# LayerNorm statistics of three blocks on ScalarE, and an earlier load of the second GLU chunk's weights, in a Trainium2 kernel

## Chip, cores and metric

The kernel runs on one core of one Trainium2 chip. The metric is the device time of one execution in microseconds. Three runs of the kernel before gave 1589.58, 1590.20 and 1592.14 us, median 1590.2. The profile is of one execution, with a span of 1589.2 us.

## The reference

A pre-norm transformer layer in float32 with 2048 tokens of 576 values: attention in 32 heads of 18, in which each token sees itself and the seven tokens 2, 4, ... 14 places before it, then a gated MLP of width 4608.

```python
def _layernorm(x, axis=-1, eps=1e-5):
    m = jnp.mean(x, axis=axis, keepdims=True)
    v = jnp.var(x, axis=axis, keepdims=True)
    return (x - m) / jnp.sqrt(v + eps)
...
    h = x + _A_ref(_layernorm(x, axis=-1), A_wqkv, A_wo)
    h2 = h + _B_ref(_layernorm(h, axis=-1), B_w_gate, B_w_up, B_w_down)
...
    # _A_ref: W, dil = 8, 2
    idx = pos[:, None] - off[None, :]
    logits = jnp.einsum("bhsd,bhswd->bhsw", q, kg) * scale
    logits = jnp.where(mask[None, None, :, :], logits, -1e9)
    attn = _softmax(logits, axis=-1)
    o = jnp.einsum("bhsw,bhswd->bhsd", attn, vg)
    return (lambda x, *d: x.transpose(*d))(o, 0, 2, 1, 3).reshape(B, S, D) @ wo
...
    # _B_ref
    h = _sigmoid(g) * u
    return jnp.einsum("bsf,fd->bsd", h, w_down)
```

## The kernel before

The tokens are cut into four blocks of 512 (even and odd tokens, first and second half of each), and each block into four tiles of 128 tokens. Matrix products are made in a float32 form of reduced precision: each operand is split into a high and a low part, and three products are summed. `split` does that: ScalarE copies the source into the high part (line 104), VectorE subtracts it from the source for the low part (line 105); `split_rest` is the same for the last 64 of the 576 values, which are stored twice (lines 108 and 109).

Stage one is norm, q, k and v, and attention. `ln1` norms the tiles of a block with `ln_j`, TensorE transposes each (`tr_main`, line 139, and `tr_rest`, line 143), and the result is split into `th` and `tl`. In `ln_j` VectorE makes mean and variance by two `bn_stats` and a `bn_aggr` and adds EPS (lines 123 to 125), GpSimd takes the power -0.5 (line 126). For blocks 0 and 1 VectorE then subtracts and scales in one instruction (line 134) and copies the last 64 values (line 135); for blocks 2 and 3 VectorE negates the mean (line 129) and ScalarE subtracts it (centring, line 130), scales (line 131) and copies (line 132). `qkv` makes, for a block and a group of eight heads, 14 products per tile of tokens (`tok_major`, lines 150 to 153), evicted by ScalarE (line 384) and written to memory by three transfers that ScalarE issues (lines 388 and 390). `norm_under` interleaves the norm of the next block with the products of the present one, in the order in which the program text emits them, shifted by priorities (`tc.high_priority`); each engine's instructions are then in a fixed queue, and an instruction that waits holds all behind it on its engine.

Attention (`att_all`) runs on VectorE: for a pass (block, head group) it loads q, k and v windows on SyncE's queue, multiplies, reduces, takes a maximum and subtracts it (lines 182 to 195), takes the exponential on ScalarE (line 196), normalizes and sums with v (lines 208 to 219). `step(ag, n)` advances it between other work. Block 0's output stays on chip; those of blocks 1 to 3 go to memory (line 221) and come back as `oj`. `front` makes block 0's projection, second norm and the GLU operands, and stores two of them (lines 503 and 505).

Stage two is the GLU: 14 single chunks and 22 paired chunks of 128 hidden values, for blocks 0 and 1 and then for 2 and 3. `single` makes two sums, pg and pu, in two of the three banks b1 to b3, takes the sigmoid of pg on ScalarE (line 653) and multiplies on VectorE (`hidden`, line 629). Weights come with `load_gu` (line 565) and are split in `weights`; chunk 0's weights `wg` are loaded earlier and split by `first_split` into the tile `wf`. Between the stages the memory pools of stage one (`ps_stk`, `sa_stk`) are closed, and those of stage two take their place. After that, chunk 1's weights are loaded on GpSimd's queue (line 979), and chunk 0's down weights are split into a `d` tile (line 981). `under_first` runs the rest of block 1's attention, and then its projection, under the first chunks.

The pool `sah` has two buffers named `h`. They hold in turn the input x of blocks 0, 1, 2 and 3, the raw q, k and v weights of the last head group, and x of block 0 again for the residual.

Of the kernel before, what the change touches and what calls it, by code (L numbers as in the profile page):

```python
# [15 lines left out]
F32 = mybir.dt.float32  # L16
F32R = mybir.dt.float32r
AF = mybir.ActivationFunctionType
ALU = mybir.AluOpType
AX = mybir.AxisListType  # L20

P = 128
S = 2048
D = 576
# [6 lines left out]
NS = 4  # L31
TB = P * NS
DM = 512
DR = D - DM
DX = D + DR
# [5 lines left out]
EPS = 1e-5  # L41
# [3 lines left out]
GU = 10 * P  # L45
WC = GU + D
# [6 lines left out]
HI = 400  # L53
# [7 lines left out]
def kernel(ctx, tc, x, wqkv, wo, wmlp, out):  # L61
# [41 lines left out]
    def split(hi, lo, src):  # L103
        act.activation(hi, src, AF.Copy)  # L104
        splits.append(dve.tensor_tensor(lo, src, f32(hi), ALU.subtract))  # L105
# [9 lines left out]
                sp.dma_start(bass.AP(tensor=a.tensor, offset=a.offset,  # L115
                                     ap=[[LP * CG // 16, 16], [1, LP * CG // 16]]), zero)

    def ln_j(xj, xn, on_act):
        bs = sm.tile([P, 2, 6], F32, bufs=4, name="bs")
        mv = sm.tile([P, 2], F32, bufs=4, name="mv")  # L120
        rstd = sm.tile([P, 1], F32, bufs=4, name="rstd")
        for k in range(2):
            dve.bn_stats(bs[:, k], xj[:, k * DH2:(k + 1) * DH2])
        dve.bn_aggr(mv, bs)
        dve.tensor_scalar(rstd, mv[:, 1:2], EPS, None, ALU.add)
        pool.tensor_tensor(rstd, rstd, mhalf, ALU.pow)
        if on_act:
            nm = sm.tile([P, 1], F32, bufs=4, name="nm")
            dve.tensor_scalar(nm, mv[:, 0:1], -1.0, None, ALU.mult)
            act.activation(xn[:, :D], xj, AF.Identity, bias=nm)  # L130
            act.activation(xn[:, :D], xn[:, :D], AF.Copy, scale=rstd)
            act.activation(xn[:, D:DX], xn[:, DM:D], AF.Copy)
        else:
            dve.tensor_scalar(xn[:, :D], xj, mv[:, 0:1], rstd, ALU.subtract, ALU.mult)
            dve.tensor_copy(xn[:, D:DX], xn[:, DM:D])

    def tr_main(ps, xn):
        for c in range(4):
# [86 lines left out]
    def step(gen, n):  # L225
        for _ in range(n):
            if next(gen, END) is END:
                return

    def drain(gen):  # L230
        for _ in gen:
            pass
# [7 lines left out]
    def proj_j(bank, t, wos, th, tl, xn_tile, put, order=(0, 1)):  # L240
        oj = t[0]
        pv = tr_main(bank(), oj)
        with tc.high_priority(HI):
            split(th[:, 0:4], tl, pv)
        yield
        pv = tr_rest(bank(), oj)
        with tc.high_priority(HI):
            split_rest(th[:, 4], pv)
        yield
        for i in order:  # L250
            ps = bank()
            tok_major(ps, DH2, th, tl, slice(0, P), *wos[i])
            hs = t[1][:, i * DH2:(i + 1) * DH2]
            with tc.high_priority(HI):
                dve.tensor_tensor(hs, hs, ps[:, :DH2], ALU.add)
            yield
        xn = xn_tile()
        with tc.high_priority(HI):
            ln_j(t[1], xn, False)
        yield  # L260
        pv = tr_main(bank(), xn)
        with tc.high_priority(HI):
            put(pv, slice(0, 4))
        yield
        pv = tr_rest(bank(), xn)
        with tc.high_priority(HI):
            put(pv.unsqueeze(1), slice(4, 5))
        yield
# [53 lines left out]
    def tok_tile(shape=(P, NS, DX)):  # L322
        return stk.tile(list(shape), F32, tag="tok", bufs=2, name="tok")
# [14 lines left out]
    def ln1(b, xb):  # L338
        th = th3_tile(F32R) if b == 3 else th_tile()
        tl = tl_tile()  # L340
        yield th, tl
        xn = tok_tile()
        for j in range(NS):
            js = slice(j * P, (j + 1) * P)
            pri = 2 * HI if b == 0 else HI if b > 1 else 0
            with tc.high_priority(pri):
                ln_j(xb[:, j], xn[:, j], b > 1)
            pv = tr_main(mm_tile(), xn[:, j])
            pr = tr_rest(acc_tile(), xn[:, j])
            with tc.high_priority(pri):  # L350
                split(th[:, 0:4, js], tl[:, :, js], pv)
                split_rest(th[:, 4, js], pr)
            yield
# [153 lines left out]
    def first_split(ws):  # L507
        wf = xt.tile([P, 20, P], F32R, tag="th", bufs=3, name="wf")
        r = ws[:, :GU].rearrange("p (c n) -> p c n", c=10)
        parts = []  # L510
        for lo, hi, c0, c1 in ((0, 10, 5, 10), (10, 14, 3, 5), (14, 20, 0, 3)):
            t = wf[:, lo:hi].rearrange("p (a c) n -> p a c n", a=2)
            split(t[:, 0], t[:, 1], r[:, c0:c1])
            parts.append(t)
        w1, w2, w4 = parts
        return dict(b00=(w1, 0), b10=(w1, 2), b01=(w2, 0), g4=(w1, 4), u4=(w4, 0), b11=(w4, 1))
# [2 lines left out]
    fr = front()  # L519
    for _ in qkv(1, 3, T[1], w[3]):  # L520
        step(ag, 1 if ready else 4)
    while not ready:
        step(ag, 1)
    more = qkv(2, 3, T[2], w[3])
# [15 lines left out]
                ww = first_split(wg)  # L540
    with tc.high_priority(HI):
        drain(fr)
    ps_stk.close()
    sa_stk.close()

# [17 lines left out]
    def load_gu(f, eng=sp, n=WC):  # L563
        ws = gw.tile([P, WC], F32, bufs=2, name="wg")
        behind[0] = eng.dma_start(ws[:, :n], wmlp[f][:, :n])
        return ws
# [5 lines left out]
    def d_tile():  # L572
        return gd.tile([P, 2, D], F32R, bufs=4, name="d")
# [401 lines left out]
    items = ([("std", 0, f) for f in range(NSTD)] + [("pair", 0, f) for f in range(NSTD, NF)]  # L975
             + [("std", 1, f) for f in range(NSTD)] + [("pair", 1, f) for f in range(NF)])
    bg = under_first()
    with tc.high_priority(2 * HI):
        wg2 = load_gu(1, pool)
        d = d_tile()  # L980
        split(d[:, 0], d[:, 1], wg[:, GU:WC])
        wc = ww, d
    wg = wg2
    seg = []

    def last_pair(i):
# [123 lines left out]
    for c, (kind, p, f) in enumerate(items):  # L1110
        w, d = wc
        for b, late_c in ((0, NF + NSTD - 3), (1, NF + NSTD + 5)):
            if c == late_c:
                e, hf = BLOCKS[b]
                paced(ov[e, hf], hacc[b])
        skip = () if kind == "std" else (3,)
        by_seven = c >= NF + NSTD
        if c == NSTD:
            finish_bg()
            last_x = splits[-1]  # L1120
            bg = under_rest(getattr(last_x, "ins", last_x))
        if c == NF + NSTD:
            finish_bg()
            with tc.high_priority(HI):
                for n in ("s1", "a11"):
                    Xn[n] = x_half(*raw[n])
            X = Xn
            pp_stk.close()
            dw = ctx.enter_context(sb_pool("dw", "right"))
        if c + 1 < len(items):  # L1130
            wc = weights(items[c + 1][0], wg, c + 1 < NF + NSTD)
        if c + 2 < len(items):
            wg = load_gu(items[c + 2][2], n=WC if c + 2 < NF + NSTD else GU)
        hid = {}
        blocks = [p] if kind == "std" else [2 * p, 2 * p + 1]

        def last(h0, h1):
            hid[0] = hidden(*h0, "h0")
            hid[1] = hidden(*h1, "h1")

        if kind == "std":
            hid = single(X, w, p, late, twice)
        elif not by_seven:
            side = last_pair if c == NF - 1 else bg_step

            def between(i):
                if i in (4, 6):
                    units(2)
                side(i)

            pair(X, w, between, last)
        else:
            def between(i):
                nonlocal st, gc, gc_bufs, dk
                units(1)
                if c == NF + NSTD and i == 5:
                    assert not queue
                    st_stk.close()
                    gc_stk.close()
                    gc = gc_stk.enter_context(sb_pool("gc2"))  # L1160
                    st = st_stk.enter_context(sb_pool("st2"))
                    dk = dk_stk.enter_context(sb_pool("dk", "right"))
                    for n in ("s4h", "s4l", "s1h"):
                        dk.tile([P, TB], F32R, name=n)
                    gc_bufs = 2
                down_side(f, i)

            pair(X, w, between, last if f >= NF - NPL else last_sums(f))
            if f < NF - NPL:
                if f % 2:  # L1170
                    if f == 1:
                        queue.append(lag(LAG))
                    queue.append(seven())
                continue
            d = M[f]
        seg.append((hid, d))
        if len(seg) == 2:
            if by_seven and f == NF - NPL + 1:
                queue.append(load_tails())
            for b in blocks:  # L1180
                queue.append(down_std(seg, b, f // 2) if kind == "std" else
                             down_tail(seg, b, f == NF - 1) if by_seven else down_units(seg, b))
            seg = []
# [44 lines left out]
```

## Time and profile before

| | us |
|---|---|
| median of the runs | 1590.2 |
| span of the profiled execution | 1589.2 |
| TensorE busy | 1553.3 |
| VectorE busy | 1268.1 |
| ScalarE busy | 869.2 |
| GpSimd busy | 184.2 |
| first product of GLU chunk 0 starts | 222.95 |

PE is TensorE's matrix products, PEld its weight loads, DVE VectorE, ACT ScalarE, POOL GpSimd, SP SyncE; a q behind the name (ACTq, SPq) marks the issue of a transfer by that engine's queue. A line such as `L609 PE MATMUL b<-tl,w` tells the line of the program, the engine, the operation, and which tile is written from which. In brackets stands how long the engine was idle before the instruction and what ended the wait. "Granted clock" is the share of TensorE's full clock that the chip granted. Matrix products overlap, so the duration of one is longer than the time from its start to the next one's start.

### The profile page before, as it was taken

How to read it: one execution, taken by the hardware profiler on the slowest of the kernel's cores; microseconds unless marked ns; L12 is line 12 of the kernel's file. 1: busy time of each engine (PE TensorE's matmuls, PEld its weight loads, DVE VectorE, ACT ScalarE, POOL GpSimd, SP SyncE). 2: the span in 40 equal slices, each digit the busy share in tenths (PEclk: the TensorE clock that was granted, in tenths of full speed). 3: DMA queues.
4: the chain of work that ended last, by engine and by line, in shares of the span. 5: the costliest groups of instructions: out<-in, count | busy, mean ns of one | idle time of the engine just before them, and what ended most of it. 6: DMA issues, size and time to landing. Idle time of an engine off the chain costs nothing.

```text
span 1589.2 us, 22383 instructions
## 1 busy us (share of the span) xinstructions
PE 1553.3 (98%) x8532; PEld 1381.6 (87%) x8532; DVE 1268.1 (80%) x1931; ACT 869.2 (55%) x1546; POOL 184.2 (12%) x230
## 2 busy tenths in 40 slices
PE   7999979999999999999989999999999999999998
PEld 6999968888888888888879988888888888888887
DVE  7999988959999999999546687876677776677755
ACT  4432234425555666656443255776677776677761
POOL 1000000011010001000101100122112112212210
PEclk9999999999999999999999999999999999999999
DMA  7664544346367565665764234899989999989983
GB/s 267 208 206 163 193 184 165 133 177 246 104 164 205 157 170 139 166 191 149 210 203 143 100 110 110 182 186 181 176 169 183 184 173 180 177 170 182 184 170 124
DMA packets 76892, 273.50 MB, mean 172 GB/s; under 512 B 8336, under 2 KB 14224, under 8 KB 75888
## 3 DMA queue, kind: packets, MB, share of 16 engines
q0 software_dynamic: 27792, 105.89, 36.3%
q1 hardware_dynamic: 41360, 146.06, 27.4%
q10 hardware_dynamic: 7632, 20.12, 3.3%
q8 instruction: 67, 1.10, 0.3%
q14 instruction: 41, 0.34, 0.1%
HBM read 145.88 MB, written 128.52 MB: 173 GB/s over the span
## 4 chain that ended last, share of the span: by engine, by line
PE 55%; issue 27%; POOL 7%; DVE 6%; DMA 4%; ACT 1%; SPq 0%; POOLq 0%; ACTq 0%; DVEq 0%
PE b L609 23%; PE dp L723 15%; POOL h L794 7%; PE acc L150 6%; PE b L616 4%; PE b L150 1%; PE bgp L150 1%; DMA wg<-in_wmlp_dram 1%; DVE pr L182 1%; DMA x<-tok 1%; DVE pr L208 1%; DVE lg L186 1%; PE acc L152 1%; DMA tail<-h 1%; PE acc L153 1%
## 5 line engine op out<-in xcount | busy, mean ns | idle before, releaser
L609 PE MATMUL b<-tl,w 128*128 128x512 f32 x1716 | 438.1, 395 | 9.1 <-ACT w L104 6.5
L609 PEld LDWEIGHTS b<-tl,w 128*128 128x128 f32 x1716 | 311.7, 189 | 66.5 <-ACT w L104 7.7
L609 PE MATMUL b<-th,w 128*128 128x512 f32 x1368 | 352.8, 393 | 0.4 <-DVE s L698 0.3
L609 PEld LDWEIGHTS b<-th,w 128*128 128x128 f32 x1368 | 249.8, 188 | 46.7 <-DVE s L698 0.7
L104 ACT ACTIVATE w<-wg 128x640 fp32r<-128x640 f32 (+2 forms) x197 | 117.0, 598 | 125.2 <-PE b L616 59.8
L791 ACT ACTIVATE ev<-dp 128x576 f32<-128x576 f32 x224 | 145.0, 647 | 61.8 <-PE dp L785 58.2
L616 PE MATMUL b<-th,w 128*128 128x512 f32 x572 | 177.0, 391 | 0.0
L794 POOL DMA_DIRECT2D h<-ev x128 | 110.2, 862 | 456.8 <-ACT ev L791 440.5
L105 DVE TENSOR_TENSOR w<-wg,w 128x640 fp32r<-128x640 f32 (+2 forms) x197 | 126.8, 649 | 38.7 <-ACT w L104 38.3
L150 PE MATMUL acc<-qw,th 128*128 128x432 f32 x512 | 155.7, 365 | 1.2 <-DVE th L109 0.9
L105 DVE TENSOR_TENSOR w<-tw,w 128x512 fp32r<-128x512 f32 x116 | 79.6, 687 | 81.1 <-ACT w L104 80.2
L616 PEld LDWEIGHTS b<-th,w 128*128 128x128 f32 x572 | 107.7, 188 | 23.1
L723 PE MATMUL dp<-d,h0h 128*128 128x288 f32 x640 | 119.0, 296 | 1.7 <-DVE tail L733 1.7
L723 PE MATMUL dp<-d,h1h 128*128 128x288 f32 x640 | 120.0, 297 | 0.0
L723 PEld LDWEIGHTS dp<-d,h0h 128*128 128x128 f32 x640 | 99.4, 189 | 5.5 <-DVE tail L733 2.0
L150 PEld LDWEIGHTS acc<-qw,th 128*128 128x128 f32 x512 | 97.2, 190 | 6.5 <-DVE th L109 1.1
L723 PEld LDWEIGHTS dp<-d,h1h 128*128 128x128 f32 x640 | 99.5, 190 | 2.9
L731 ACT ACTIVATE stage<-dp 128x576 f32<-128x576 f32 x96 | 61.7, 646 | 62.4 <-PE dp L723 62.3
L104 ACT ACTIVATE w<-tw 128x512 fp32r<-128x512 f32 x116 | 72.8, 628 | 41.3 <-PE b L609 40.9
L150 PE MATMUL acc<-qw,tl 128*128 128x432 f32 x256 | 92.8, 362 | 0.0
L384 ACT ACTIVATE ev<-acc 128x432 f32<-128x432 f32 x64 | 33.9, 531 | 104.4 <-PE acc L153 97.7
L182 DVE TENSOR_TENSOR pr<-kw,q 128x2304 f32<-128x2304 f32 x32 | 81.7, 2552 | 2.8 <-DMA kw<-k 2.6
(278 smaller groups left out, 2899.8 us busy)
## 6 DMA issues: line engine op xcount, KB each, us to landing
h<-ev POOLq DMA_DIRECT2D x96, 576.0 KB, 7.2
wg<-in_wmlp_dram SPq DMA_DIRECT2D x49, 928.0 KB, 5.2
h<-stage POOLq DMA_DIRECT2D x24, 1152.0 KB, 10.6
wg<-in_wmlp_dram SPq DMA_DIRECT2D x36, 640.0 KB, 4.1
kw<-k SPq DMA_DIRECT2D x16, 792.0 KB, 4.4
vw<-v SPq DMA_DIRECT2D x16, 792.0 KB, 5.5
wd<-in_wmlp_dram SPq DMA_DIRECT2D x18, 576.0 KB, 7.2
h<-ev POOLq DMA_DIRECT2D x32, 288.0 KB, 6.8
```

The source lines that it names most:

```text
L104: act.activation(hi, src, AF.Copy)
L105: splits.append(dve.tensor_tensor(lo, src, f32(hi), ALU.subtract))
L150: pe.matmul(ps[:, :n], a[:, c, js], m[:, c], start=k == 0, stop=False)
L152: pe.matmul(ps[:, :n], th[:, 4, js], wh[:, 4], start=False, stop=False)
L182: dve.tensor_tensor(pr, both(kw, u), q[:, us].unsqueeze(2).broadcast_to([P, 2, W, CG]), ALU.mult)
L384: act.activation(ev[:, :, j], ps[:, :NQ].rearrange("p (t c) -> p t c", t=3), AF.Copy)
L609: pe.matmul(ps, wt[:, a, k0 + c], xx[:, m + c], start=first and k == 0, stop=k == 5, skip_group_check=True)
L616: pe.matmul(ps, wt[:, a, k0], xx[:, 4], start=False, stop=a == 1, skip_group_check=True)
L723: pe.matmul(ps[:, i, :DH2], a[:, js], d[:, m, i * DH2:(i + 1) * DH2], start=k == 0, stop=k == n)
L731: act.activation(hv, ps, AF.Copy)
L791: act.activation(hs[:, k % 2], ps[:, :, :DH2], AF.Copy)
L794: pool.dma_start(hsev[:, u, k0:k + 1], hs[:, :k + 1 - k0], accum_op=ALU.add, max_dma_last_dim=8 * D)
```

## The change

Two parts. In the first, `ln_j` keeps only the form in which VectorE does all, and is used for block 0 and for the second norm. Blocks 1, 2 and 3 take `ln_stats` and `ln_scale`: ScalarE copies x scaled by -1/576 with a sum over the row (the accumulator output), which is the negative mean; adds it to x; squares the result with a sum, which is the variance, and writes the squares over x; GpSimd adds EPS and takes the power; ScalarE scales and copies the last values. Statistics are emitted one tile ahead of the scaling. In the second, chunk 1's weights are loaded into an `h` buffer by SyncE, before the rest of block 0's work; both chunks' gate and up weights and both down weights are split before the pools are changed (`first_split`, `first_down`), and the load on GpSimd's queue is gone.

```diff
-    def ln_j(xj, xn, on_act):
+    def ln_j(xj, xn):
...
-        if on_act:
-            nm = sm.tile([P, 1], F32, bufs=4, name="nm")
-            dve.tensor_scalar(nm, mv[:, 0:1], -1.0, None, ALU.mult)
-            act.activation(xn[:, :D], xj, AF.Identity, bias=nm)
-            act.activation(xn[:, :D], xn[:, :D], AF.Copy, scale=rstd)
-            act.activation(xn[:, D:DX], xn[:, DM:D], AF.Copy)
-        else:
-            dve.tensor_scalar(xn[:, :D], xj, mv[:, 0:1], rstd, ALU.subtract, ALU.mult)
-            dve.tensor_copy(xn[:, D:DX], xn[:, DM:D])
+        dve.tensor_scalar(xn[:, :D], xj, mv[:, 0:1], rstd, ALU.subtract, ALU.mult)
+        dve.tensor_copy(xn[:, D:DX], xn[:, DM:D])
+
+    def ln_stats(xj, xn):
+        mv = sm.tile([P, 2], F32, bufs=4, name="mv")
+        nm, var = mv[:, 0:1], mv[:, 1:2]
+        rstd = sm.tile([P, 1], F32, bufs=4, name="rstd")
+        act.activation(xn[:, :D], xj, AF.Copy, scale=-1.0 / D, accum_out=nm)
+        act.activation(xn[:, :D], xj, AF.Identity, bias=nm)
+        act.activation(xj, xn[:, :D], AF.Square, scale=D ** -0.5, accum_out=var)
+        pool.tensor_scalar(rstd, var, EPS, None, ALU.add)
+        pool.tensor_tensor(rstd, rstd, mhalf, ALU.pow)
+        return rstd
+
+    def ln_scale(rstd, xn):
+        act.activation(xn[:, :D], xn[:, :D], AF.Copy, scale=rstd)
+        act.activation(xn[:, D:DX], xn[:, DM:D], AF.Copy)
...
     def ln1(b, xb):
...
+        pri = 2 * HI if b == 0 else HI if b > 1 else 0
+        rstd = []
+
+        def stats(n):
+            with tc.high_priority(pri):
+                for j in range(len(rstd), n):
+                    rstd.append(ln_stats(xb[:, j], xn[:, j]))
+
         for j in range(NS):
             js = slice(j * P, (j + 1) * P)
-            pri = 2 * HI if b == 0 else HI if b > 1 else 0
+            if b:
+                stats(min(j + 2, NS))
             with tc.high_priority(pri):
-                ln_j(xb[:, j], xn[:, j], b > 1)
+                if b:
+                    ln_scale(rstd[j], xn[:, j])
+                else:
+                    ln_j(xb[:, j], xn[:, j])
...
     for _ in qkv(1, 3, T[1], w[3]):
         step(ag, 1 if ready else 4)
+    with tc.high_priority(HI):
+        wg1 = sah.tile([P, NS, D], F32, bufs=2, name="h").rearrange("p j d -> p (j d)")[:, :WC]
+        sp.dma_start(wg1, wmlp[1])
...
     with tc.high_priority(HI):
         drain(fr)
+
+    def first_down(ws):
+        d = xt.tile([P, 2, D], F32R, tag="tl", bufs=4, name="df")
+        split(d[:, 0], d[:, 1], ws[:, GU:WC])
+        return d
+
+    with tc.high_priority(HI):
+        wc = ww, first_down(wg)
+        wc_next = first_split(wg1), first_down(wg1)
     ps_stk.close()
     sa_stk.close()
...
-    with tc.high_priority(2 * HI):
-        wg2 = load_gu(1, pool)
-        d = d_tile()
-        split(d[:, 0], d[:, 1], wg[:, GU:WC])
-        wc = ww, d
-    wg = wg2
...
-        if c + 1 < len(items):
+        if c == 0:
+            wc = wc_next
+        elif c + 1 < len(items):
             wc = weights(items[c + 1][0], wg, c + 1 < NF + NSTD)
```

More of the change, by code (lines that the diff above doesn't have):

```diff
@@ L258, in proj_j @@
         with tc.high_priority(HI):
-            ln_j(t[1], xn, False)
+            ln_j(t[1], xn)
         yield
```

## The prediction

> **What bounds the kernel now.** I read the busy table first, then the stretches, then the list of TensorE's waits.
>
> ```profile
> PE 1553.3 (98%) x8532; PEld 1381.6 (87%) x8532; DVE 1268.1 (80%) x1931; ACT 869.2 (55%) x1546; POOL 184.2 (12%) x230
> ```
>
> TensorE works 1553.3 of 1589.2 us and the change takes no matmul away, so a gain can come only from the 36 us in which it stands still, and from stretches in which it works at a lower clock. The stretches (columns: length, then busy time and instructions of TensorE, weight loads, VectorE, ScalarE, GpSimd; granted clock; DMA share; GB/s):
>
> ```profile
> 30.00:40.00 10.00, 10.00 (x59) 9.40 (x58) 6.28 (x23) 8.72 (x20) 2.62 (x5) 1.00 0.98 343
> 40.00:50.00 10.00, 9.14 (x54) 8.49 (x53) 9.72 (x29) 6.75 (x16) 2.20 (x4) 1.00 0.90 322
> 50.00:184.00 134.00, 133.74 (x695) 127.37 (x694) 128.54 (x119) 42.40 (x92) 0.91 (x1) 1.00 0.53 183
> 223.00:236.00 13.00, 6.51 (x29) 5.02 (x27) 8.63 (x5) 3.85 (x6) 1.33 (x2) 0.86 0.93 353
> 236.00:249.00 13.00, 10.46 (x30) 8.01 (x31) 9.09 (x13) 5.45 (x10) 0.00 (x0) 0.62 0.22 73
> 320.00:324.00 4.00, 4.00 (x23) 3.70 (x21) 2.05 (x3) 1.20 (x2) 0.00 (x0) 0.63 1.05 405
> 400.00:780.00 380.00, 380.00 (x2091) 336.49 (x2091) 362.22 (x455) 223.08 (x366) 32.65 (x31) 1.00 0.62 161
> ```
>
> From 30 to 40 us TensorE is never idle and ScalarE, where the change puts work, is already busy 8.72 of 10 us. From 50 to 184 both TensorE (133.74 of 134) and VectorE (128.54) are full: a delay of TensorE ahead of this stretch is not made good in it, and less work on VectorE doesn't shorten it. From 223 to 249, the passage to the GLU stage, TensorE has 9 us of idle and a clock of 0.62. From 400 to 780 it is never idle, so a shift that stands at 400 goes to the end. The waits between 200 and 330 us (us in all, times, longest):
>
> ```profile
> PE b L609 <- ACT w L104: 6.5, 1, 6.5
> PE b L609 <- DVE s L629: 2.5, 1, 2.5
> PE b L139 <- DMA oj<-o: 2.4, 1, 2.4
> ```
>
> The first two are the passage; the third is block 1's projection, which waits until its attention has been written out and read back.
>
> **Part one, the norm on ScalarE.** What VectorE loses: its group of the first 60 us (count, busy us and mean ns), then the views of the tiles mv and rstd (least, median and most ns of one):
>
> ```profile
> L123 DVE BATCH_NORM_STATS2 bs<-h 128x6 f32<-128x288 f32 x32 | 13.1, 437 | 4.5 <-DMA h<-in_x_dram 4.4
> ```
>
> ```profile
> L124 DVE BATCH_NORM_AGGREGATE mv<-bs x16: 151/200/209, 4.6 to 44.9; 128x2 f32<-128x12 f32 x16
> ```
>
> ```profile
> L125 DVE TENSOR_SCALAR rstd<-mv x16: 135/145/156, 5.0 to 45.8; 128x1 f32<-128x1 f32 x16
> L126 POOL TENSOR_TENSOR rstd<-rstd,mhalf x16: 549/552/822, 5.3 to 46.0; 128x1 f32<-128x1 f32 x16
> L134 DVE TENSOR_SCALAR tok<-h,mv,rstd x8: 562/575/580, 8.4 to 32.5; 128x576 f32<-128x576 f32 x8
> L131 ACT ACTIVATE tok<-tok,rstd x8: 764/774/778, 33.1 to 53.5; 128x576 f32<-128x576 f32 x8
> ```
>
> 24 x 0.437 + 12 x 0.200 + 20 tiny ones x 0.145 + block 1's 4 x 0.575 = 18.1 us, and block 1's four small copies. This is off TensorE's path (VectorE's stretch above); its worth is that block 1's attention ends earlier.
>
> ScalarE's queue is worked strictly in order, so what counts is where the 36 added activations stand. The rows that give the prices:
>
> ```profile
> 41.08 0.33 ACTq L388 DMA_DIRECT2D q<-ev  x1
> 41.44 0.45 ACTq L390 DMA_DIRECT2D k<-ev  x1
> 41.93 0.47 ACTq L390 DMA_DIRECT2D v<-ev  x1
> 43.56 0.53 ACT L384 ACTIVATE ev<-acc 128x432 f32<-128x432 f32 x1 [2.03 <-PE acc L153]
> 43.99 0.60 ACT L104 ACTIVATE th<-mm 128x512 fp32r<-128x512 f32 x1
> 44.49 0.27 ACT L108 ACTIVATE th<-acc 128x128 fp32r<-128x128 f32 x1
> 44.65 1.44 ACT L130 ACTIVATE tok<-h,nm 128x576 f32<-128x576 f32 x2
> ```
>
> One 128x576 activation has its result after 0.77 (L131) and holds the queue for 0.67, since two in a row end after 1.44. From start to start an eviction holds it 0.43, a wide split 0.50, a narrow one 0.16, and the three issues of q, k and v 1.3 (41.08 to the end of 41.93 + 0.47). TensorE at the same time:
>
> ```profile
> 36.75 0.60 PE L139 MATMUL mm<-ident,tok 128*128 128x128 f32 x4
> ...
> 40.05 0.60 PE L139 MATMUL mm<-ident,tok 128*128 128x128 f32 x4
> ```
>
> The transposes at 36.75 and 40.05 are those of block 1's third and fourth tile. Now they wait for nothing, because VectorE normed them early. In the changed order they wait for ScalarE's scaling.
>
> Third tile. Its scaling stands behind the eviction of the very product that ends as these transposes begin, with a square of block 2, a wide split and two narrow ones between: 0.43 + 0.67 + 0.16 + 0.50 + 0.16 + 0.77 = 2.7 after it, and I add 0.5 for the hand-overs from TensorE to ScalarE and back, an estimate: TensorE idles 3.2. The copy to the last 64 columns comes behind one more activation: 0.3.
>
> Fourth tile. After the next 14 matmuls ScalarE has, between their eviction and the scaling that the transposes want: the eviction 0.43, a scaling of block 2 0.67, the three DMA issues 1.3, a copy 0.16, a centring 0.67, a narrow split 0.16, a square 0.67, the scaling 0.77: 4.8, with 0.3 for the hand-overs 5.1 of idle. Its last-columns copy stands behind one more scaling of block 2: 0.7. Behind the waiting scaling stand the splits that VectorE's halves need, so nothing overtakes.
>
> Clock. After the idle of 2.4 us the trace grants 0.63 for 4 us (320 to 324): 4 x 0.37 = 1.5 us lost. Twice: 3.0. Together 3.2 + 0.3 + 5.1 + 0.7 + 3.0 = 12.3; the 0.9 that TensorE stands still now between 40 and 50 falls in the same place and goes: 11.4. For small waits of blocks 2 and 3, and for the fourth weight group's split, which slips in VectorE's order against TensorE, I take 1.5 (bounds 0 and a whole 2.55 product of attention, as the passage below shows it).
>
> Not shown by this trace: an activation with an accumulator output (24 of them) and GpSimd's addition of EPS. An accumulator's extra lies between 0 and 0.27, a whole narrow activation (44.49 above); about six lie on the chain of each of the two stalls. I take 0.1 each, 1.0 in all; bounds 0 and 3. The addition ahead of the power costs up to another 0.55 on GpSimd (L126); it is covered as long as ScalarE's own chain is later, which it is at both stalls. Part one puts the end of qkv later by 11.4 + 1.5 + 1.0 = 13.9, bounds 8 and 19.
>
> **Part two, the passage.**
>
> TensorE, then ScalarE, then VectorE (start, us):
>
> ```profile
> 222.95 1.56 PE L609 MATMUL b<-tl,wf 128*128 128x512 f32 x6
> ...
> 236.03 1.22 PE L609 MATMUL b<-tl,w 128*128 128x512 f32 x2 [6.52 <-ACT w L104]
> ```
>
> ```profile
> 232.36 0.68 ACT L104 ACTIVATE d<-wg 128x576 fp32r<-128x576 f32 x1 [8.68 <-DMA x<-tok]
> 232.37 0.33 ACTq L390 DMA_DIRECT2D v<-ev  x1
> 233.06 1.28 ACT L653 ACT_TABLE_LOAD   x1
> 234.36 0.60 ACT L653 ACTIVATE s<-b 128x512 f32<-128x512 f32 x1
> ```
>
> ```profile
> 223.60 2.55 DVE L182 TENSOR_TENSOR pr<-kw,q 128x2304 f32<-128x2304 f32 x1
> 226.19 2.55 DVE L186 TENSOR_REDUCE lg<-pr 128x128 f32<-128x2304 f32 x1
> ...
> 243.12 0.61 DVE L194 TENSOR_REDUCE mx<-lg 128x32 f32<-128x256 f32 x1
> ...
> 244.32 0.41 DVE L195 TENSOR_TENSOR lg<-lg,mx 128x256 f32<-128x256 f32 x1
> ```
>
> Chunk 0 takes 222.95 to 229.5 (236.03 - 6.52), 6.5 us. Chunk 1 needs as much and a wait of 2.5 follows in it. In the stretch from 236 TensorE is busy 10.46 of 13 at a clock of 0.62, and little more than a chunk's worth of products is done in it: 13 - 6.5 = 6.5 lost there, 2.5 of it idle and about 4 to the clock; with the 6.5 before it 13.0 are lost. The weights come by GpSimd's queue and their split stands on ScalarE behind a down-weight split that waits for a store (8.68).
>
> Changed, chunk 1's weights and both down splits are ready before. The bank of its first product is still held until chunk 0's sigmoid has read it, and that is late next: in ScalarE's new order it stands behind the exponential of attention's pass (1, 2), which stands behind VectorE's second product, reduce, maximum and subtraction, and these come after the new down splits. From about 1.6 after chunk 0's start (two splits of 0.75): 2.55 + 2.55 + 0.61 + 0.41, the exponential some 0.4 (an estimate: half as many elements a row as a 512 split, whose row is at 0.60), table 1.28, sigmoid 0.60 = 8.4, so 10.0; TensorE is done at 6.5 and idles 3.5, then loses between 1.5 and 4 at the lower clock; I take 2.3, nearer the single wait of 320: 5.8 in place of 13.0. Gain 7.2, bounds 4 (if the hidden multiply behind VectorE's long product, 2.55, is waited for as well) and 9. The early load waits on SyncE's queue for the raw weights of the last head group to be split, and the loads of attention's next q, k and v stand behind it; VectorE has work from the pass before, so I count nothing, at worst part of one 2.55 product.
>
> **Later.** VectorE has 18 us less to do and TensorE reaches block 1's projection about 7 later: the wait of 2.4 for the attention's last output, and the 1.5 of low clock after it, go: 3.9 (bounds 0 and 3.9).
>
> The Trainium skill, "TensorE: Matmul & The Clock Gate", section "What's actually happening", says that the clock halves only after an idle window of about 3.4 us. By that rule the 2.4 us wait would cost no clock, and the gain here would be 2.4, the whole 1.5 worse. The trace disagrees, 0.63 after 2.4 us of idle, and I go by the trace.
>
> **Sum.** Against the profiled 1589.2: + 13.9 - 7.2 - 3.9 = + 2.8, and + 1.0, part of one 2.55 product, because the evictions of q, k and v come later on ScalarE, so attention's first loads too, and its first product stands ahead of block 1's splits on VectorE: 1593.0. The median of the runs stands 1.0 above the profile's span: 1594.0.
>
> **Rivals.** (a) The norm keeps ahead: the hardware's order leaves ScalarE enough slack that the third tile's scaling is done in time, and only half of the early loss comes. For it: ScalarE idles 2.03 before 43.56. Against: that idle is a wait for TensorE's product, which the scaling would stand behind too. With 5 instead of 14.9: 1590.2 + 5 - 11.1 = 1584; with no loss at all 1579. Chance 0.22. (b) It cancels: early loss of 9 to 13 with the gains as worked out, 1588 to 1593. Chance 0.25. (c) Forecast, 1593.4 to 1599: chance 0.33. (d) Slower by more: each accumulator holds ScalarE's queue for the full 0.27 and the next step waits for it; it decides once both stalls are longer by some 2 us. Early loss 19, the passage gains only 4, the rest 3.9: 1590.2 + 19 - 7.9 = 1601. For it: ScalarE is at 8.72 of 10 where the work is added. Against: it idles at the start of the stretch. Chance 0.20. That the weights aren't early after all is excluded by the order: the load stands ahead of attention's pass (0, 3) on SyncE.
>
> **Numbers.** A measurement tells 0.2% (3.2 us) from no change. Faster is (a), 0.22; same is (b), 0.25; slower (c) and (d), 0.53. The range 1583 to 1604 takes in most of (a) and (d), and (c) alone is 1593 to 1599.
>
> **What would show it.** Waits of TensorE's transposes for ScalarE's scaling of about 3 and 5 us between 36 and 52; the start of chunk 0 near 237; one wait of about 3.5 for chunk 0's sigmoid in place of 6.5 and 2.5; no wait for oj. Wrong would be no wait before 50 us, or a long one for the hidden multiply after 240.

## The result and the profile after

The changed kernel took 1601.48 us (median of 5 runs, 1595.12 to 1604.14) against 1590.23 us before (5 runs, 1589.58 to 1592.14): ratio 1.0062, 95% interval 1.0044 to 1.0081, slower by 11.2 us. It also spreads more, 9 us against 2.6. The forecast was 1594, with a range of 1583 to 1604: the sign and the range hold, the size is off by 7.5 us. The profiled execution (1603.51 us, the second longest of the five) has a span of 1601.6 us, 12.4 more than before.

The busy table:

```profile
PE 1558.2 (97%) x8532; PEld 1385.1 (86%) x8532; DVE 1256.3 (78%) x1867; ACT 887.1 (55%) x1604; POOL 191.0 (12%) x241
```

VectorE lost 11.8 us of work net, ScalarE gained 17.9. TensorE is busy 4.9 us longer with the same matmuls, and the stretches show where its clock was lower; the other 7.5 us of the 12.4 are idle time. The stretches (columns as before):

```profile
36.00:54.00 18.00, 10.19 (x36) 8.27 (x35) 15.99 (x16) 14.35 (x36) 3.58 (x10) 0.72 0.74 266
54.00:80.00 26.00, 21.89 (x114) 20.10 (x114) 21.91 (x23) 17.32 (x45) 9.56 (x8) 0.93 0.37 127
80.00:146.00 66.00, 66.00 (x343) 63.20 (x342) 63.30 (x62) 21.43 (x46) 0.94 (x1) 1.00 0.49 177
146.00:200.00 54.00, 52.94 (x270) 50.33 (x270) 40.00 (x37) 12.58 (x26) 0.00 (x0) 1.00 0.55 196
200.00:234.00 34.00, 30.76 (x198) 29.19 (x197) 31.27 (x60) 7.77 (x21) 2.45 (x4) 0.95 0.47 167
```

Where TensorE had no idle from 30 to 40, it now stands still for 7.8 of 18 us at a clock of 0.72, for another 4.1 up to 80, and for 1.1 and 3.2 later on the way to the GLU. The timeline of TensorE names what ended these waits:

```profile
39.43 0.65 PE L147 MATMUL mm<-ident,tok 128*128 128x128 f32 x4 [3.02 <-ACT tok L142]
...
49.30 1.12 PE L147 MATMUL mm<-ident,tok 128*128 128x128 f32 x4 [4.43 <-ACT tok L142]
...
67.67 0.60 PE L158 MATMUL acc<-qw,th 128*128 128x432 f32 x1 [1.33 <-ACT ev L404]
...
74.85 0.47 PE L158 MATMUL acc<-qw,th 128*128 128x432 f32 x1 [1.97 <-ACT ev L404]
...
147.84 0.66 PE L158 MATMUL acc<-qw,th 128*128 128x432 f32 x2 [1.06 <-DVE qw L105]
...
206.55 0.40 PE L158 MATMUL mm<-wo,th 128*128 128x288 f32 x1 [2.62 <-DVE tl L105]
...
244.00 1.55 PE L641 MATMUL b<-tl,wf 128*128 128x512 f32 x6
...
254.38 1.95 PE L641 MATMUL b<-tl,wf 128*128 128x512 f32 x6 [3.85 <-ACT s L685]
...
262.47 0.62 PE L641 MATMUL b<-tl,w 128*128 128x512 f32 x2
...
319.80 0.66 PE L147 MATMUL b<-ident,oj 128*128 128x128 f32 x4 [0.33 <-DMA oj<-o]
```

L142 is the scaling in `ln_scale`, L404 the eviction of q, k and v, L685 the sigmoid. Chunk 0 starts at 244.00 instead of 222.95: 21.05 us lost. Chunk 2 starts at 262.47; before it was 248.81:

```profile
248.81 0.84 PE L609 MATMUL b<-tl,w 128*128 128x512 f32 x3
```

So the passage takes 18.5 us instead of 25.9 and gives 7.4 back. Of the 21.05 us, 13.7 are then still missing. By the end of the span another 1.3 are regained; the wait for oj is among these gains (0.33 instead of 2.40).

### The profile page after: what moved, and what is told of

Same layout as the page of the kernel before. It is cut to its first block, busy times and chain, and to the rows that moved or that the text cites. A ratio compares the mean times of both kernels' runs of the same rounds, so it can differ in the third digit from the quotient of the medians.

```text
span 1601.6 us, 22374 instructions
## 1 busy us (share of the span) xinstructions
PE 1558.2 (97%) x8532; PEld 1385.1 (86%) x8532; DVE 1256.3 (78%) x1867; ACT 887.1 (55%) x1604; POOL 191.0 (12%) x241
## 4 chain that ended last, share of the span: by engine, by line
PE 80%; DVE 10%; DMA 5%; ACT 2%; issue 1%; POOL 1%; SPq 0%; ACTq 0%; DVEq 0%; POOLq 0%
PE b L641 40%; PE dp L755 14%; PE dp L817 11%; PE b L648 7%; PE acc L158 3%; DVE lg L194 2%; DMA wg<-in_wmlp_dram 1%; DVE pr L216 1%; DVE pr L190 1%; PE b L158 1%; PE bgp L158 1%; DMA kw<-k 1%; DMA ar<-x 1%; DVE w L105 1%; DVE pr L222 1%
## 5 line engine op out<-in xcount | busy, mean ns | idle before, releaser
L641 PE MATMUL b<-tl,w 128*128 128x512 f32 x1704 | 431.3, 393 | 0.0
L641 PEld LDWEIGHTS b<-tl,w 128*128 128x128 f32 x1704 | 308.1, 188 | 55.2 <-DVE s L661 0.3
L641 PE MATMUL b<-th,w 128*128 128x512 f32 x1356 | 349.2, 392 | 1.8 <-DVE s L730 1.7
L641 PEld LDWEIGHTS b<-th,w 128*128 128x128 f32 x1356 | 246.7, 188 | 47.5 <-DVE s L730 2.1
L104 ACT ACTIVATE w<-wg 128x384 fp32r<-128x384 f32 (+2 forms) x194 | 115.4, 598 | 119.5 <-PE b L648 60.1
L158 PE MATMUL acc<-qw,th 128*128 128x432 f32 x512 | 159.5, 373 | 5.2 <-ACT ev L404 4.1
L105 DVE TENSOR_TENSOR w<-wg,w 128x384 fp32r<-128x384 f32 (+2 forms) x194 | 125.3, 651 | 37.9 <-ACT w L104 37.5
L648 PEld LDWEIGHTS b<-th,w 128*128 128x128 f32 x568 | 106.7, 188 | 23.3
L755 PE MATMUL dp<-d,h0h 128*128 128x288 f32 x608 | 112.5, 295 | 0.8 <-DVE tail L765 0.8
L190 DVE TENSOR_TENSOR pr<-kw,q 128x2304 f32<-128x2304 f32 x32 | 81.7, 2554 | 24.6 <-DMA kw<-k 24.3
L755 PEld LDWEIGHTS dp<-d,h0h 128*128 128x128 f32 x608 | 93.6, 189 | 3.8 <-DVE tail L765 1.0
L404 ACT ACTIVATE ev<-acc 128x432 f32<-128x432 f32 x64 | 33.9, 530 | 94.5 <-PE acc L161 90.8
```

The lines of the kernel that those rows point to most:

```text
L158: pe.matmul(ps[:, :n], a[:, c, js], m[:, c], start=k == 0, stop=False)
L190: dve.tensor_tensor(pr, both(kw, u), q[:, us].unsqueeze(2).broadcast_to([P, 2, W, CG]), ALU.mult)
L404: act.activation(ev[:, :, j], ps[:, :NQ].rearrange("p (t c) -> p t c", t=3), AF.Copy)
L641: pe.matmul(ps, wt[:, a, k0 + c], xx[:, m + c], start=first and k == 0, stop=k == 5, skip_group_check=True)
L648: pe.matmul(ps, wt[:, a, k0], xx[:, 4], start=False, stop=a == 1, skip_group_check=True)
L755: pe.matmul(ps[:, i, :DH2], a[:, js], d[:, m, i * DH2:(i + 1) * DH2], start=k == 0, stop=k == n)
```

## The experiments

Each time is a median of its runs, each ratio stands against runs of the kernel before taken with it. Their median is 1589.16 for early_weights_only, norm_only, block1_first and eps_in_square (one instruction on GpSimd); 1589.56 for block1_on_vector, block1_on_vector_eps (the same with one instruction), three_gpsimd and early_weights_held (early weights and the order on VectorE); and 1589.76 for before_held, changed_held (that order on the kernels before and changed) and best_norm. "Chunk 0" and "chunk 2" are the starts of their first products in the profiled execution, which is one execution of each kernel. Such starts differ between executions: changed_held (below) has TensorE's products in the same order as the changed kernel up to chunk 0, and its chunk 0 starts at 240.73, 3.3 us earlier than 244.00. The changed kernel's wait of 2.62 us at 206.55 is missing there.

### The early weights alone

The kernel before with the second part of the change only: `wg1`, `first_down` and `wc_next` as in the diff above, `ln_j` and `ln1` untouched.

> The norm as in the kernel before, chunk 1's weights and both down splits early as in the changed one. Theory A: the passage gains about 7.3 us (chunk 2 starts some 18.5 us after chunk 0 instead of 25.9), but block 1's attention is no earlier on VectorE except for the 4.3 us of idle that VectorE has in the passage before, so the wait for oj grows from 2.4 to some 4 to 6 us: 1586 to 1588. Rival B, the passage's gain is whole whatever VectorE does: 1582 to 1583. Rival C, the oj wait takes all of it: 1590.

1583.27 us (1581.79 to 1583.61), ratio 0.9957 (0.9945 to 0.9970). Chunk 0 starts at 222.96 as before, chunk 2 at 242.91: the passage takes 19.9 us, a gain of 5.9, 1.4 short of the 7.3 expected. TensorE's timeline of this kernel, and VectorE's:

```profile
237.05 2.92 PE L621 MATMUL b<-tl,wf 128*128 128x512 f32 x6 [4.38 <-DVE s L641]
```

```profile
230.59 2.55 DVE L182 TENSOR_TENSOR pr<-kw,q 128x2304 f32<-128x2304 f32 x1
233.06 0.75 DVE L105 TENSOR_TENSOR df<-h,df 128x576 fp32r<-128x576 f32 x1
233.73 2.55 DVE L186 TENSOR_REDUCE lg<-pr 128x128 f32<-128x2304 f32 x1
236.31 0.69 DVE L641 TENSOR_TENSOR s<-s,b 128x512 f32<-128x512 f32 x1
```

Here the sigmoid was in time, and the hidden multiply of chunk 0 (L641) was late: it stands on VectorE behind a product, a split and a reduce of attention. The wait for oj was 2.2 us, as before, not longer as theory A had it, and the time fell to rival B's figure: 1583. The passage's gain came through to the end without any relief on VectorE.

### The norm alone

The changed kernel with the weights loaded and split as before, by GpSimd's queue after the pool change.

> The norm statistics on ScalarE as changed, chunk 1's weights on GpSimd's queue after the pool change as before. Theory A: chunk 0 starts some 21 us later than before, the passage costs its 25.9 us as before (waits of about 6.5 and 2.5), the wait for oj goes (3.9): about 1590 + 21 - 4 = 1607. Rival: the late start is made good in part in the passage, because VectorE is ahead: 1600 or less.

1603.98 us (1601.85 to 1604.36), ratio 1.0086 (1.0073 to 1.0100). Chunk 0 starts at 241.35 and chunk 2 at 261.3, so the passage took 20.0 us and not 25.9, with a wait of 3.9 for the weights where before it was 6.5: part of the late start is made good there even without the early load. The wait for oj was 3.15 us: VectorE's relief (12.4 us less busy than before) did not remove it. The time lies between the two expectations. The norm costs 14.8 us alone; the early load is worth 5.9 us alone, and by the medians only 2.5 on top of the norm (1603.98 to 1601.48), which is inside the spread of the changed kernel's runs.

### Block 1 ahead in ScalarE's queue

```diff
-        pri = 2 * HI if b == 0 else HI if b > 1 else 0
+        pri = HI if b > 1 else 2 * HI
```

> As changed, with the norm of block 1 at block 0's priority (the same instructions in another order on ScalarE). Theory A, the order on ScalarE's queue costs the third and fourth tile's waits: they go, chunk 0 starts about 11 us earlier than in the changed kernel (near 233), and the time is about 1592 (10 off, 1 to 2 given back at oj). Rival, it is the amount of ScalarE's work, not its order: the waits come for other instructions and the time stays within 3 us of the changed kernel's 1601.

1597.17 us (1593.97 to 1597.68), ratio 1.0042 (1.0029 to 1.0054): between the two. The waits of the third and fourth tile are gone: nothing over 0.6 us until 62, and the order was their cause. Others took their place:

```profile
62.68 0.66 PE L147 MATMUL mm<-ident,tok 128*128 128x128 f32 x4 [3.05 <-ACT tok L142]
...
194.34 0.69 PE L147 MATMUL mm<-ident,tok 128*128 128x128 f32 x2 [2.48 <-DVE tok L227]
...
199.52 0.88 PE L151 MATMUL acc<-ident,tok 128*128 128x128 f32 x3 [4.06 <-DVE tok L429]
```

The first is a tile of a later block, whose scaling is late in its turn; the other two are block 0's attention, whose output (L227, L429) now comes later than TensorE wants it. Chunk 0 starts at 237.44, 6.6 us earlier than in the changed kernel, not 11.

### Block 1 back on VectorE

```diff
-            if b:
+            if b > 1:
                 stats(min(j + 2, NS))
...
-                if b:
+                if b > 1:
                     ln_scale(rstd[j], xn[:, j])
```

> As changed, with block 1 normed by VectorE as before; blocks 2 and 3 keep their statistics on ScalarE, and chunk 1's weights are early. Theory A, what costs is ScalarE's queue under block 1, and GpSimd held by VectorE's products under blocks 2 and 3: no waits of 3 and 4.4 us between 36 and 52, the start of chunk 0 near 232 (9 later than before instead of 21), 1588 to 1592. Rival, blocks 2 and 3 lose as much in any order: 1597 or more.

1600.60 us (1598.31 to 1601.56), ratio 1.0066 (1.0053 to 1.0080): the rival's case. Chunk 0 starts at 242.18, not near 232. Block 1's norm was early, but what follows it waits:

```profile
44.46 0.47 PE L158 MATMUL acc<-qw,th 128*128 128x432 f32 x1 [4.20 <-ACT th L104]
50.28 1.11 PE L147 MATMUL mm<-ident,tok 128*128 128x128 f32 x4 [5.36 <-DVE tl L105]
```

On ScalarE the splits of block 1 have no raised priority and stand behind the statistics of block 2, which have it. From 27.99 to 43.83 that queue holds evictions, transfers and nothing but block 2's norm, and the first split of block 1 comes at 43.83. The second wait, 5.36, is for VectorE's half of that split: it starts at 49.54, behind a reduce, a product and a reduce of attention that fill VectorE from 41.77 on. In each of these three orders (changed, block 1 first, block 1 on VectorE) the norm's chain on ScalarE delays something TensorE needs next.

### One, two and three instructions on GpSimd

ScalarE's scaling waits for GpSimd, and the cause shows in the changed kernel's timelines of GpSimd, VectorE and ScalarE:

```profile
49.05 0.57 POOL L138 TENSOR_TENSOR rstd<-rstd,mhalf 128x1 f32<-128x1 f32 x1
...
60.55 2.40 POOL L137 TENSOR_SCALAR rstd<-mv 128x1 f32<-128x1 f32 x1 [1.56 <-ACT h L136]
63.04 0.57 POOL L138 TENSOR_TENSOR rstd<-rstd,mhalf 128x1 f32<-128x1 f32 x1
...
70.49 2.12 POOL L137 TENSOR_SCALAR rstd<-mv 128x1 f32<-128x1 f32 x1 [2.42 <-ACT h L136]
```

```profile
47.58 2.55 DVE L194 TENSOR_REDUCE lg<-pr 128x128 f32<-128x2304 f32 x1
...
60.32 2.56 DVE L216 TENSOR_TENSOR pr<-vw,lg 128x2304 f32<-128x2304 f32 x1
...
69.98 2.56 DVE L190 TENSOR_TENSOR pr<-kw,q 128x2304 f32<-128x2304 f32 x1
```

```profile
60.52 0.67 ACT L134 ACTIVATE tok<-h 128x576 f32<-128x576 f32 x1
61.09 0.19 ACT L134 ACTIVATION_READ_ACCUMULATOR tok<-h 128x1 f32 x1
61.19 0.51 ACT L404 ACTIVATE ev<-acc 128x432 f32<-128x432 f32 x1
63.64 0.78 ACT L142 ACTIVATE tok<-tok,rstd 128x576 f32<-128x576 f32 x1 [1.94 <-POOL rstd L138]
...
64.95 0.77 ACT L135 ACTIVATE tok<-h,mv 128x576 f32<-128x576 f32 x1
65.62 0.25 ACT L143 ACTIVATE tok<-tok 128x64 f32<-128x64 f32 x1
...
73.30 0.77 ACT L142 ACTIVATE tok<-tok,rstd 128x576 f32<-128x576 f32 x1 [2.24 <-POOL rstd L138]
...
74.28 0.52 ACT L404 ACTIVATE ev<-acc 128x432 f32<-128x432 f32 x1
```

GpSimd's addition over 128 values took 2.40 us: it ended with the VectorE product that had started just before it (60.32 + 2.56 = 62.88; 60.55 + 2.40 = 62.95). The next one, 2.12 us long, did the same (69.98 + 2.56 = 72.54; 70.49 + 2.12 = 72.61). Under a reduce of the same length (47.58 to 50.13) the power took its 0.57. ScalarE waited 1.94 and 2.24 for the results, with the splits and evictions behind: the eviction at 74.28 is the one for which TensorE waits 1.97 us at 74.85. The Trainium skill, "SBUF — State Buffer", section "Who interferes with whom", says that a VectorE instruction with two inputs in SBUF contends with GpSimd's reads, that the one issued first keeps the other out for its whole length, and that a reduce never contends. The trace agrees: 2.40 and 2.12 us behind products, 0.57 under a reduce. To price it, one kernel has one instruction a tile and one has three:

```diff
+    beps = cst.tile([P, 1], F32, name="beps")
+    pool.memset(beps, (EPS / D) ** 0.5)
...
-        act.activation(xj, xn[:, :D], AF.Square, scale=D ** -0.5, accum_out=var)
-        pool.tensor_scalar(rstd, var, EPS, None, ALU.add)
-        pool.tensor_tensor(rstd, rstd, mhalf, ALU.pow)
+        act.activation(xj, xn[:, :D], AF.Square, bias=beps, scale=D ** -0.5, accum_out=var)
+        pool.tensor_tensor(rstd, var, mhalf, ALU.pow)
```

> As changed, without GpSimd's addition: EPS comes as a bias of sqrt(EPS/576) into the square, whose sum over a centred row is then the variance plus EPS. One GpSimd instruction a tile instead of two. Theory A, GpSimd's small instructions are held while VectorE's 2.55 us products run and ScalarE's scaling waits for them (1.67, 1.94 and 2.24 us in the changed kernel): about half of the 6 us that chunk 0's start loses between 54 and 80 us goes, 1597 to 1599. Rival, the evictions there are late only because ScalarE has more to do: no change, 1601.

```diff
-        pool.tensor_scalar(rstd, var, EPS, None, ALU.add)
+        pool.tensor_scalar(rstd, var, EPS / 2, None, ALU.add)
+        pool.tensor_scalar(rstd, rstd, EPS / 2, None, ALU.add)
```

> As changed, with EPS added in two halves by two GpSimd instructions: three a tile instead of two. Theory A, each of them can be held by a running VectorE product, and ScalarE's scaling waits for it: chunk 0 starts 3 to 6 us later than in the changed kernel and the time is 1604 to 1607. Rival, they cost their own 0.2 us on an idle engine: the same 1601 within 1.

One instruction: 1598.88 us (1595.74 to 1600.08), chunk 0 at 238.54. Three: 1603.26 (1602.21 to 1606.01), chunk 0 at 243.22. The medians go the way of theory A, 2.6 less and 1.8 more than the changed kernel's 1601.48, but its own runs reach from 1595 to 1604, so neither step alone is clear of the spread, and three instructions didn't start chunk 0 later than two (244.00). One against three is clear: 4.4 us, without overlap, or 2.2 us an instruction, less than I had set. The hold is shown by the rows. That it alone makes the 4.4 us is not: from 54 to 80 us TensorE idles 3.5, 4.1 and 4.4 us with one, two and three instructions, and the granted clock is 1.00, 0.93 and 0.83, so most of the difference there is clock. One instruction is held too: in that kernel the power at 67.76 takes 1.97 us, and TensorE waits 3.47 for an eviction that stands behind it on ScalarE.

With block 1 back on VectorE, where GpSimd's instructions for blocks 2 and 3 were not held up to 70 us (0.22 for each addition, 0.57 for each power), the same step does nothing:

> As block1_on_vector, with EPS as a bias in the square, so that GpSimd has one instruction a tile. Theory A: 2 to 3 us less than block1_on_vector. Rival, GpSimd's instructions don't matter: the same time as block1_on_vector.

1599.93 us (1599.06 to 1601.25) against 1600.60: no difference, the rival's figure, and it fits the hold: what is not held costs nothing. (In the profiled executions chunk 0 starts 2.1 us earlier, at 240.06; the idle time from 54 to 80 us is about the same, 3.3 and 3.5 us, and the clock is 1.00 instead of 0.91.)

### The order on VectorE in the passage

Attention's second product of pass (1, 2) waits until chunk 0's hidden multiply has been issued:

```diff
+    opened = []
...
         for u in range(2):
             us = slice(2 * u, 2 * u + 2)
+            held = (b, g, u) == (1, 2, 1)
+            while held and not opened:
+                yield
             pr = at.tile([P, 2, W, CG], F32, name="pr")
-            dve.tensor_tensor(pr, both(kw, u), q[:, us].unsqueeze(2).broadcast_to([P, 2, W, CG]),
-                              ALU.mult)
+            with ExitStack() as way:
+                if held:
+                    way.enter_context(tc.issue_after(getattr(opened[0], "ins", opened[0])))
+                dve.tensor_tensor(pr, both(kw, u),
+                                  q[:, us].unsqueeze(2).broadcast_to([P, 2, W, CG]), ALU.mult)
...
     def hidden(sg, ps, name):
-        dve.tensor_tensor(sg, sg, ps, ALU.mult)
+        opened.append(dve.tensor_tensor(sg, sg, ps, ALU.mult))
```

On top of the early weights alone:

> As early_weights_only, with attention's second product of pass (1, 2) held on VectorE until chunk 0's hidden multiply is done. In early_weights_only TensorE idled 4.4 us for that multiply, which stood behind a product and a reduce of 2.55 us each. Theory A: the idle and its low clock go (chunk 2 starts some 15 to 16 us after chunk 0 instead of 19.9), the held product and reduce come later for oj, whose wait grows from 2.2 to 4 or 5: 1580 to 1582. Rival, VectorE's sum of work decides and the order only shifts where TensorE waits: 1583, as early_weights_only.

1575.49 us (1574.21 to 1577.50), ratio 0.9912 (0.9899 to 0.9926): 14 us faster than before and the fastest of all. More than theory A gave. TensorE passes from chunk to chunk with one short wait:

```profile
235.49 0.61 PE L635 MATMUL b<-th,wf 128*128 128x512 f32 x2
236.56 1.67 PE L628 MATMUL b<-tl,w 128*128 128x512 f32 x6 [0.45 <-ACT s L672]
```

```profile
313.83 0.66 PE L139 MATMUL b<-ident,oj 128*128 128x128 f32 x4 [0.66 <-DMA oj<-o]
```

Chunk 2 starts 13.4 us after chunk 0 (223.20 to 236.56), which is two chunks of 6.4 and little else; the wait for oj did not grow, it fell to 0.66. On the kernel before, and on the changed one:

> The kernel before with attention's second product of pass (1, 2) held until chunk 0's hidden multiply, and nothing else. Theory A, early weights and the order on VectorE need each other: chunk 1 still waits 6.5 for its weights, during which the multiply is done anyway, so only the wait of 2.5 can go: 1586 to 1590. Rival, the order on VectorE alone made the 8 us between early_weights_only and early_weights_held: 1581 or less.

> As changed, with the same product held. In the changed kernel TensorE idled 3.85 us for chunk 0's sigmoid, which stood on ScalarE behind the exponential of that pass. Theory A: the exponential comes after the sigmoid, the idle and its low clock go, chunk 2 starts 14 us after chunk 0 instead of 18.5: 1595 to 1598; what the norm costs is then the difference to early_weights_held, some 20 us. Rival, VectorE's load makes another wait of the same size in its place: 1601.

Before with the hold alone: 1589.00 us (12 runs, 1586.51 to 1591.55), ratio 0.9994 (0.9985 to 1.0003), no difference: the wait for weights, 6.9 us, stays, the one of 2.5 goes, and the wait for oj is 3.4 instead of 2.4. Changed with the hold: 1594.89 (11 runs, 1591.43 to 1598.63), ratio 1.0031 (1.0018 to 1.0043); the wait for the sigmoid is gone and chunk 2 starts 12.7 us after chunk 0. Against early_weights_held the norm then costs 19.4 us. Both times came as theory A had it, the second's passage 1.3 us shorter than put there.

### The norm with all that helped

> The norm statistics on ScalarE with all that helped so far: block 1's norm at block 0's priority, EPS in the square, chunk 1's weights early, the product held. Theory A, statistics on ScalarE cost more than VectorE's relief is worth in any of these orders: 1585 to 1592, at least 10 slower than early_weights_held. Rival, with the waits gone the relief of 18 us on VectorE pays: 1576 or less.

1590.54 us (12 runs, 1587.62 to 1593.52), ratio 1.0007 (0.9997 to 1.0017): as fast as before, and 15 us slower than early_weights_held. Its chunk 0 starts at 238.37, 15.2 us after that of early_weights_held: the whole difference is made before the GLU. With block 1 first the waits are those of block1_first again: 2.87 us for a scaling at 63.71, 2.46 and 4.52 for block 0's attention at 194.92 and 200.10.

## Why the prediction was right, and where it was wrong

**Which way, and by which terms.** The bound was read rightly: what is lost before 50 us isn't made good up to chunk 0, and less work on VectorE bought nothing there. The relief was also smaller than worked out: 18.1 adds up durations of small instructions that overlap in the trace, and the busy table shows 11.8. Nor could it be used. The keys of attention's first pass came no earlier than before (its first product started at 35.95 there), and with the norm's work gone VectorE stood waiting for them:

```profile
37.12 2.56 DVE L190 TENSOR_TENSOR pr<-kw,q 128x2304 f32<-128x2304 f32 x1 [11.51 <-DMA kw<-k]
```

It waited 11.51 us there and 12.81 more at 168.24, 24.3 together, against 2.6 before. In block1_first and best_norm its largest waits up to 235 us are for ScalarE's half of the splits instead, 17.3 and 24.6 together. So the direction was no luck: what the norm saved on VectorE was spent waiting. That the time lies within the range is luck in part: it is outside the forecast case (c), and 2.5 us from the range's upper end, which was set for case (d).

**Third and fourth tile: right.** Idle of 3.2 and 5.1 was worked out, 3.02 and 4.43 came, ended by ScalarE's scaling. With the lower clock and the saved 0.9, 11.4 was put in. The transposes that come next after all this, before and after:

```profile
47.78 0.60 PE L139 MATMUL mm<-ident,tok 128*128 128x128 f32 x4
```

```profile
58.42 0.60 PE L147 MATMUL mm<-ident,tok 128*128 128x128 f32 x4
```

They are 10.6 us later, and the last product ahead of both stalls was 0.5 earlier (36.55 and 36.05): 11.1. In block1_first, which only moves these instructions, both waits vanish. The 1.0 added at the end, for attention's first product ahead of block 1's splits, is not seen: the product is there (37.12, with a split at 39.71 behind it), but no wait of TensorE between 36 and 54 us is put down to VectorE.

**"Small waits of blocks 2 and 3, and the fourth weight group's split: 1.5": wrong, and this is the step that failed.** 21.05 - 11.1 leaves 10 us, where 1.5 were put in. The stretches show 9.7 of them: 4.1 us of idle and 7% of clock (1.8) from 54 to 80, 1.1 at the weight split, 3.2 idle and 5% of clock (1.7) from 200 to 234, where before 2.2 of idle stood between 184 and 223. The largest wait of the last stretch, 2.62 us at 206.55, is for a split on VectorE at 205.81 that stands behind a reduce, a maximum and a subtraction of attention; changed_held's execution does not have it. What I missed between 54 and 80 is that ScalarE's chain goes through GpSimd a second time, where VectorE's products run. I had written that the addition costs 0.55 at most and is covered at both stalls. At the stalls it was: neither of the two scalings (38.58 and 48.48) waited for GpSimd. Behind them it took up to 2.40, and ScalarE waited 1.67, 1.94 and 2.24. In this trace TensorE's three waits from 54 to 80 (0.81, 1.33 and 1.97, all of the 4.1) stand behind the second and third of these. But block1_on_vector, where nothing is held, idles 3.5 us in the same stretch, so it isn't shown that they would go without the hold.

**Accumulators: they cost nothing that the trace shows.** Each adds a row ACTIVATION_READ_ACCUMULATOR of 0.19 us, and the next instruction starts 0.10 after it (61.09 to 61.19). But the activation with the sum is itself shorter, 0.67 against 0.77: it holds the queue for 0.67 with its read (60.52 to 61.19), as one without a sum does (64.95 to 65.62). 0.1 each, 1.0 in all, was taken, within bounds of 0 and 3.

**The passage: right.** Gain 7.2 worked out, 7.4 measured, with the sigmoid behind the exponential as named:

```profile
252.00 0.42 ACT L204 ACTIVATE lg<-lg 128x256 f32<-128x256 f32 x1 [7.28 <-DVE lg L203]
...
253.73 0.60 ACT L685 ACTIVATE s<-b 128x512 f32<-128x512 f32 x1
```

Its end was put 10.0 us after chunk 0's start, and it came 10.3 after (253.73 + 0.60 - 244.00), with a wait of 3.85 for 3.5. But it was right for the changed kernel only. With the norm as before the same early load gives 5.9, since the multiply is late instead, and without any early load the late start of norm_only gains as much. The two parts are not additive.

**oj: the wait went, half of the reason was wrong, and less was left of it.** It fell to 0.33. I gave two reasons, that VectorE has 18 us less to do and that TensorE comes later. Before, the row was

```profile
319.78 0.66 PE L139 MATMUL b<-ident,oj 128*128 128x128 f32 x4 [2.40 <-DMA oj<-o]
```

and in the changed kernel it starts at 319.80: attention's output came back at the same time as before, and TensorE got there 2.1 us later. So the second reason carried it. That VectorE's relief brings the output earlier is not borne out by any like pair of runs. TensorE's first product on oj starts at 323.60 in norm_only and at 319.78 before, at 319.80 in the changed kernel and at 312.68 in early_weights_only, at 329.08 in changed_held and at 313.83 in early_weights_held: with the norm on ScalarE it is later each time. At the place itself the gain is about what was worked out, 2.1 of idle and 1.7 of clock (0.83 and 1.00 granted from 320 to 330 us). But the changed kernel has other waits around it, of 0.56, 0.82 and 0.45 us up to 335, and of the 3.9 only 1.3 stand at the end of the span.

**Rivals.** (d), the slower one, met the time (1601), by its own route only in part: the loss ahead of chunk 0 was 21 against the 19 it assumed, but the passage gained all its 7.4, and the accumulators did not hold the queue for 0.27.

**Open.** What share of the loss from 54 to 80 us is GpSimd's hold and what share ScalarE's queue; why the changed kernel spreads over 9 us. The traces of changed and changed_held show that one order of instructions can have the wait at 206 us or not, but not why.

## What to carry to other kernels

A queue that is worked in order has two loads: how much it does and what stands in it just ahead of what the busiest engine wants. ScalarE was 55% busy here, yet a chain of statistics put ahead of evictions and splits cost 14 to 19 us in every order tried, and the engine it relieved spent the time waiting. Moving one early load and then the one instruction that was late next gave 14 us together; the second gave nothing without the first. Before a small operation goes to GpSimd, look at what VectorE runs at that time.

## What the runs showed of the hardware

TensorE's clock fell after waits that are each shorter than the 2.4 us that the trace of before showed. In the changed kernel waits of 0.81 and 1.33 us within 2 us were followed by products at half rate:

```profile
66.01 0.33 PE L151 MATMUL acc<-ident,tok 128*128 128x128 f32 x1 [0.81 <-DVE th L109]
67.67 0.60 PE L158 MATMUL acc<-qw,th 128*128 128x432 f32 x1 [1.33 <-ACT ev L404]
68.07 0.56 PE L158 MATMUL acc<-qw,tl 128*128 128x432 f32 x1
68.43 0.92 PE L158 MATMUL acc<-qw,th 128*128 128x432 f32 x2
69.15 0.56 PE L158 MATMUL acc<-qw,tl 128*128 128x432 f32 x1
...
71.29 0.36 PE L158 MATMUL acc<-qw,tl 128*128 128x432 f32 x1
```

From 67.67 to 71.29 a product takes 0.56 us and the next one starts 0.36 later, afterwards 0.36 and 0.20: 3.6 us at about half speed after two waits that make 2.1 together, with a granted clock of 0.54 from 67.6 to 71.3. A single wait of 1.97 us, at 74.85, was not followed by slow products (granted clock 1.00 from 74.8 to 77). These traces give no rule for waits of this length.
